# One more feature group by seven products, its first differences on VectorE, and two moved steps, in a fused attention and GLU kernel

## The chip, the cores and the metric

The kernel runs on one core of a Trainium2 chip. The metric is the device time of one execution in microseconds, lower is better. The engines are called by the profile's names: PE (TensorE matmuls), DVE (VectorE), ACT (ScalarE), POOL (GpSimd) and SP, whose queue issues most of the transfers.

## The reference

```python
# x 2048 x 640; wqkv 640 x 1920; wo 640 x 640; w_gate, w_up 640 x 1536; w_down 1536 x 640
xn = layernorm(x)
q, k, v = heads(xn @ wqkv)                  # 32 heads of 20
idx = pos[:, None] - 2 * arange(8)          # 8 taps, two positions apart
a = softmax(where(idx >= 0, q . k[idx] / sqrt(20), -1e9))
s = (sum over taps of a * v[idx]) @ wo
g = silu(((xn @ w_gate) * (xn @ w_up)) @ w_down)
out = x + s * g
```

All of it is fp32.

## The kernel before

**Products.** An fp32 product is three fp32r matmuls: both operands are split into a high part (ACT copies it to fp32r) and a low part (POOL or DVE subtracts it: `split`, L114 and L115), and high x high, high x low and low x high are added. The normalized x lies transposed in `xT[chunk]`, four chunks of 512 positions, five blocks of 128 rows. Weights of gate and up come in 12 feature groups of 128.

**Plain and by seven products.** A plain gate and up for one feature group and one chunk (`gate_up`, L124) is 30 matmuls of 128x128 by 512. `group(f, c0, second)` (L1292) takes gate and up for the pair of chunks c0 and c0 + 1 together by a 2x2 scheme with seven products instead of eight, on four of the five blocks of x, with the fifth added: 54 matmuls, in the order j = 0, 5, 2, 1, 4, 3, 6 with 6, 9, 6, 9, 6, 9, 9 of them. It needs sums and differences on both sides. On x's side these are T1 to T4 for chunks 2 and 3 (`differences(0)` and `differences(1)`, lines L1162 to L1167, on POOL, and `last_difference`, L1188); those of chunks 0 and 1 were made earlier and stored (t_scr and e_scr, loaded again at L1148 and L1152). On the weights' side they are S1 to S4 and d5: `w_add` (L1238, POOL) and `w_split` for the blocks G, S, R, U (640, 768, 384 and 384 columns, ACT and POOL), each in one buffer that the group before must have left. The weights themselves come by `load_wf` (L180, SP).

After a product, ACT's `hold` (L1261) copies its bank where the next product adds to it; DVE adds the other banks to what was held: gate_a (L1274), gate_b (L1264), up_a (L1277); up_b (L1267) and h_b (L1270) are between two held tiles, on DVE for chunks 2 and 3 of feature groups from `VEC` = 2 on, otherwise on POOL. The result h goes to memory (L1250).

**Order.** Every engine runs its instructions in the order in which the code is written. First come layernorm, the transposes, the q, k, v products of the first head group and some gate and up; then the products of the other head groups (L434); then the groups for f = 2 to 10, each for chunks 2 and 3 and then for 0 and 1; f = 11 goes by a group for chunks 0 and 1 and plain for 2 and 3 (f = 0 and 1 are plain on all chunks, two of these products between the first and the second head group). Then `pair_product` (L996) makes s from the attention output and wo, and `product` (L866) the down projection. `places` and `beside` are tables that hang steps behind the n-th product of a group.

**Attention** on 32 heads in 12 units of head group and half runs beside the products: DVE multiplies q by the keys of a tap (L542), reduces (L549), does the softmax with ACT's exponential (L571), multiplies by the values (L508), and POOL or DVE adds (L514). It is a generator which `advance` draws on: each stretch of products grants a credit, each step of attention costs some, and what is granted sets where in the written order its instructions stand. The credit is not a time. Whatever is left at the place `beside[(10, 0, 5)]`, behind the sixth product of the group for f = 10 on chunks 2 and 3, is written out there at once by `advance(1e9)`. Behind it the output goes to memory (`store_o`, L590), the output weights are loaded (`load_wo`, L703), summed by DVE (`sums_wo`, L906 to L909) and split by ACT and POOL (`split_wo`).

**The last stage.** `product(m)` needs sums of h (`sum_h`, L813 to L821), their high and low parts (`hi_h`, `lo_h`, L829), made by DVE and ACT a few products ahead, and DVE gathers what a product gives (`gather`, L882, L886, L889).

Of the kernel before, what the change touches and what calls it, by code (L numbers as in the profile page):

```python
# [29 lines left out]
TPC = CH // P  # L30
# [26 lines left out]
def kernel(  # L57
# [1059 lines left out]
    early_high(1)  # L1117
# [7 lines left out]
    split_wq(1, nc.gpsimd)  # L1125
    gate_up(1, 2)
    gate_up(0, 3)
    gate_up(1, 3)

    f0, f1 = KF - 2, KF - 1  # L1130
    F_TWO = 2
# [24 lines left out]
    def differences(k):  # L1156

        def x(ch, a, m):
            return xT[ch][a][:, 2 * m + k, :].bitcast(F32)

        def sums(out, u, v, eng=nc.gpsimd.tensor_sub):
            eng(out, u, v)  # L1162
            yield

        def parts(j, y):
            nc.scalar.activation(t_unit(j, 0, k), y, AF.Copy)
            nc.gpsimd.tensor_sub(t_unit(j, 1, k), y, t_unit(j, 0, k).bitcast(F32))  # L1167
            yield
# [4 lines left out]
        yield from sums(a, a, x(2, 1, 0))  # L1173
        yield from parts("T1", a)
        r1 = st([P, CH], "gh", 5)
        yield from sums(r1, x(3, 0, 1), x(3, 1, 1), nc.gpsimd.tensor_add)
        yield from sums(r0, r1, r0)
        yield from parts("T3", r0)
        yield from sums(r1, r1, a)
        yield from parts("T2", r1)  # L1180
        z = t4[k] = st([P, CH], "gh", 5)
        yield from sums(z, x(2, 0, 1), r1)
        yield from sums(z, z, x(2, 1, 1), nc.gpsimd.tensor_add)
# [69 lines left out]
    def group(f, c0=0, second=0):  # L1253
# [31 lines left out]
        for n, j in enumerate((0, 5, 2, 1, 4, 3, 6)):  # L1285
# [11 lines left out]
            if (second, n) == (1, 6) and (second, n) in places:  # L1297
                places.pop((second, n))(f)
# [45 lines left out]
    def first_parts():  # L1344
        for name in ("S1", "S2", "S3", "d5", "S4"):
            w_add(2, name)
            yield
        w_split(2, "S")
        yield
# [6 lines left out]
    for m, t in ((m, t) for m in range(1, len(MADE)) for t in range(DIL)):  # L1356
# [3 lines left out]
        for i in range(NE):  # L1360
            n = t * NE + i
            if m < last and n == 0:
                load_wq(m + 1, ((0, 2), (2, 4)) if broad else ((0, 3), (3, 5)))
            elif m < last and n in BLOCK:
                split_wq(m + 1, nc.gpsimd, (BLOCK.index(n), BLOCK.index(n) + 1))
            elif broad and n == BLOCK[1] + 1:
                load_wq(m + 1, ((4, 5),))
            if (m, r, i) == (last - 1, 1, 6):
                load_wf(2)
            if (m, n) in W_SUMS:  # L1370
                wd_sum(W_SUMS.index((m, n)))
            qkv(m, r, i)
            if m == last and n == NT - 7:
                staged[:] = [y for y in staged if y is not stage_pk[-1]]
            elif m == last and n == NT - 5:
                load_t(0)
            elif m == last and n == NT - 3:
                w_split(2, "G")
# [13 lines left out]
    w_split(2, "R")  # L1392
    w_sum.pop(2)
    load_wf(3)
# [160 lines left out]
    for m in range(n_prod):  # L1555
# [5 lines left out]
        if m == 1:  # L1561
            hi_h(AHEAD)
            lo_h(AHEAD)
        elif m == 2:
# [5 lines left out]
        after()  # L1570
        if m + AHEAD + 1 < n_prod:
# [55 lines left out]
```

## Time and profile before

| | |
|---|---|
| median of 3 runs | 738.52 us (736.95 to 738.75) |
| the profiled execution | 737.74 us, of which its span is 735.7 |
| clock granted to PE | 0.999 of full speed |
| PE busy | 729.2 us, 99% of the span |
| DVE, POOL, ACT busy | 629.1, 449.4, 301.0 us |
| q, k, v of the second head group begin on PE | 105.0 us |
| the first seven-product group begins | 272.2 us |
| the last one ends | 505.6 us |

A row of a timeline gives the start, the busy time and the engine, then line, operation and tiles; where the engine was idle before it, the idle time and what ended it stand in brackets at the end. "x6" is six instructions that follow each other. Rows of groups of instructions give their count, then busy us and the mean ns of one, then idle time before them.

### The profile page before, as it was taken

To read this page: it belongs to the slowest core of one execution; us is meant where nothing else is said; L and a number is where in the kernel's file an instruction comes from. 1 tells how busy PE (TensorE), PEld (TensorE's weight loads), DVE (VectorE), ACT (ScalarE), POOL (GpSimd) and SP (SyncE) were. 2 spreads that over 40 slices of the span, in tenths; PEclk is the share of its full clock that TensorE was granted. 3 is DMA by queue.
4 is the path that set the end of the run, shared out by engine and by line. 5 is a ranking of instruction groups with operands and counts; after the bars stand their busy time and mean duration, and the time that the engine had idled before them with its cause. 6 is when DMAs were issued, how large, how long until landed. Compare 5 with 4: busy or idle time off the path is not lost.

```text
span 735.7 us, 11056 instructions
## 1 busy us (share of the span) xinstructions
PE 729.2 (99%) x4030; PEld 666.0 (91%) x4030; DVE 629.1 (86%) x729; ACT 301.0 (41%) x561; POOL 449.4 (61%) x383
## 2 busy tenths in 40 slices
PE   9999999999999999999999999999999999999997
PEld 7989989988999998888888887888999999999997
DVE  7676998799796989899989999978899897777775
ACT  5668312323232333233323332334556664444442
POOL 6159919997778889797889969667644630000000
PEclk9999999999999999999999999999999999999999
DMA  8464589889766659461733542277768955555534
GB/s 325 169 204 164 214 291 302 245 257 257 183 192 174 217 194 349 123 198 58 220 92 96 180 143 73 64 229 192 215 201 244 313 221 193 193 193 194 194 108 143
DMA packets 106436, 143.78 MB, mean 195 GB/s; under 512 B 23080, under 2 KB 75556, under 8 KB 106382
## 3 DMA queue, kind: packets, MB, share of 16 engines
q1 hardware_dynamic: 88654, 121.13, 51.8%
q10 hardware_dynamic: 16000, 12.78, 5.4%
q0 software_dynamic: 1728, 9.18, 5.2%
q8 instruction: 31, 0.51, 0.3%
q14 instruction: 23, 0.19, 0.1%
HBM read 94.40 MB, written 55.67 MB: 204 GB/s over the span
## 4 chain that ended last, share of the span: by engine, by line
PE 94%; DVE 3%; issue 1%; POOL 1%; DMA 1%; SPq 0%; ACT 0%; POOLq 0%; DVEq 0%
PE g L1292 15%; PE q L434 11%; PE u L1292 10%; PE u L434 8%; PE g L434 8%; PE q L866 8%; PE u L866 5%; PE q L1292 5%; PE g L124 5%; PE u L124 5%; PE q L996 3%; PE e L866 3%; PE g L866 3%; PE u L996 2%; PE e L996 2%; PE e L434 1%
## 5 line engine op out<-in xcount | busy, mean ns | idle before, releaser
L514 POOL TENSOR_TENSOR o<-o,t 128x960 f32<-128x960 f32 (+1 forms) x66 | 132.8, 2012 | 9.4 <-DVE t L508 8.5
L508 DVE TENSOR_TENSOR t<-e,kv 128x960 f32<-128x960 f32 (+1 forms) x96 | 99.6, 1038 | 16.2 <-POOL o L514 16.2
L542 DVE TENSOR_TENSOR t<-q,kv 128x1920 f32<-128x1920 f32 (+1 forms) x48 | 92.5, 1927 | 3.2 <-DMA kv<-qkv_scr 3.1
L549 DVE TENSOR_REDUCE lg<-t 128x96 f32<-128x1920 f32 (+1 forms) x48 | 92.3, 1924 | 0.2
L434 PE MATMUL q<-s,xc 128*128 128x360 f32 (+1 forms) x450 | 82.9, 334 | 0.1
L1261 ACT ACTIVATE gh<-g 128x512 f32<-128x512 f32 x57 | 34.1, 598 | 112.8 <-PE g L1292 108.0
L115 POOL TENSOR_TENSOR s<-wraw,s 128x384 fp32r<-128x384 f32 (+6 forms) x57 | 68.4, 1214 | 17.9 <-ACT s L114 17.8
L434 PEld LDWEIGHTS q<-s,xc 128*128 128x128 f32 x450 | 74.9, 188 | 4.2 <-ACT xc L314 0.3
L434 PE MATMUL u<-s,xc 128*128 128x360 f32 (+1 forms) x360 | 65.8, 334 | 0.0
L434 PEld LDWEIGHTS u<-s,xc 128*128 128x128 f32 x360 | 60.3, 188 | 2.2
L434 PE MATMUL g<-s,xc 128*128 128x360 f32 (+1 forms) x330 | 61.5, 338 | 0.0
L434 PEld LDWEIGHTS g<-s,xc 128*128 128x128 f32 x330 | 55.7, 188 | 2.6
L1292 PE MATMUL g<-s,s 128*128 128x512 f32 x228 | 58.0, 390 | 0.0
L1292 PE MATMUL u<-xc,s 128*128 128x512 f32 x228 | 57.9, 389 | 0.0
L866 PE MATMUL q<-xc,s 128*128 128x320 f32 x342 | 55.6, 310 | 0.6 <-DVE s L886 0.6
L866 PEld LDWEIGHTS q<-xc,s 128*128 128x128 f32 x342 | 51.5, 188 | 0.8 <-ACT s L847 0.8
L1292 PEld LDWEIGHTS g<-s,s 128*128 128x128 f32 x228 | 42.7, 188 | 9.2 <-ACT gh L1261 0.4
L1292 PEld LDWEIGHTS u<-xc,s 128*128 128x128 f32 x228 | 42.8, 188 | 8.9
L114 ACT ACTIVATE s<-wraw 128x384 fp32r<-128x384 f32 (+6 forms) x58 | 32.6, 581 | 30.3 <-PE g L1292 10.2
L1292 PE MATMUL g<-xc,s 128*128 128x512 f32 x171 | 42.0, 390 | 0.3 <-ACT gh L1261 0.3
L1292 PE MATMUL q<-xc,pk 128*128 128x512 f32 x171 | 41.9, 389 | 0.0
L514 POOL TENSOR_TENSOR o<-t 128x960 f32<-128x960 f32 (+1 forms) x11 | 22.2, 2014 | 28.3 <-DVE t L508 24.9
(332 smaller groups left out, 1561.3 us busy)
## 6 DMA issues: line engine op xcount, KB each, us to landing
h_scr<-gh SPq DMA_DIRECT2D x48, 256.0 KB, 2.6
wraw<-in_wgu SPq DMA_DIRECT2D x11, 640.0 KB, 4.5
kv<-qkv_scr SPq DMA_DIRECT2D x14, 480.0 KB, 5.9
t<-h_scr SPq DMA_DIRECT2D x8, 768.0 KB, 6.2
qkv_scr<-s ACTq DMA_DIRECT2D x17, 360.0 KB, 3.9
kv<-qkv_scr SPq DMA_DIRECT2D x14, 367.5 KB, 6.8
s_scr<-gh SPq DMA_DIRECT2D x16, 320.0 KB, 3.8
gh<-s_scr SPq DMA_DIRECT2D x16, 320.0 KB, 3.9
```

Of the source, the lines that this page charges most:

```text
L114: nc.scalar.activation(hi, raw, AF.Copy)
L115: eng.tensor_sub(lo, raw, hi.bitcast(F32))
L124: nc.tensor.matmul(acc, a, b, start=first and n == 0, stop=last and n == len(runs) - 1)
L434: nc.tensor.matmul(p, xT[(r * NE + i) // TPC][a][:, k, t0:t0 + P], wq[m][b][k], start=n == 0, stop=n == len(runs) - 1, skip_group_check=ac ...
L508: nc.vector.tensor_mul(t.rearrange("p (n d) -> p n d", d=DH), e[:, :, w].unsqueeze(2).to_broadcast([P, NE * nh, DH]), v)
L514: return NE * c * cost, lambda: eng.tensor_add(y, z, t)
L542: nc.vector.tensor_mul(t, q, k)
L549: nc.vector.tensor_reduce(out=lg[:, :, j:j + 2].rearrange("p n a -> p a n"), in_=t.rearrange("p a (n d) -> p a n d", d=DH), op=ALU.add, ax ...
L866: nc.tensor.matmul(p, y[:, i, k], wd_part(name, k, l), start=new and r == 0, stop=r == len(runs) - 1, skip_group_check=True)
L996: nc.tensor.matmul(b, y, w, start=new and r == 0, stop=r == len(runs) - 1, skip_group_check=True)
L1261: nc.scalar.activation(kept[j], b["ACACABA"[j]], AF.Copy)
L1292: nc.tensor.matmul(y, w, x, start=j in (0, 1, 5) and r == 0, stop=r == len(runs) - 1, skip_group_check=True)
```

## The change

Feature group 1 leaves the plain products on chunks 2 and 3 and is done there by `group(1, 2)`, ahead of all other groups; on chunks 0 and 1 it stays plain. So `F_TWO` is 1, and the sums, splits and loads that went with f = 2 go with f = 1. This first group has no second one on chunks 0 and 1 beside it, so what prepares f = 2 hangs behind the seven products of this one alone (`one_places`). The eleven operations of `differences(0)` go from POOL to DVE, and each takes 0.25 of attention's credit; `differences(1)` stays on POOL. The splits of the second q, k, v weights, the load of the third and the casts of `early_high(1)` stand within the first head group's second half, at its sixth product. In the last stage, `sum_h(8)` and `lo_h(7)` go from behind product 3 to behind product 4's own steps, so that the gathering of product 4 stands ahead of them on DVE.

```diff
-    early_high(1)
...
     for i in range(TPC, NE):
         qkv(0, 1, i)
         advance(PACE * 1.9)
-    split_wq(1, nc.gpsimd)
-    gate_up(1, 2)
+        if i == TPC + 1:
+            split_wq(1, nc.gpsimd)
+            load_wq(2, ((0, 2), (2, 4)))
+            early_high(1)
     gate_up(0, 3)
-    gate_up(1, 3)
+    wf_raw.clear()
...
-    F_TWO = 2
+    F_TWO = 1
...
+        eng = nc.gpsimd if k else nc.vector
+        def high(j, y):
+            nc.scalar.activation(t_unit(j, 0, k), y, AF.Copy)
+        def low(j, y):
+            eng.tensor_sub(t_unit(j, 1, k), y, t_unit(j, 0, k).bitcast(F32))
+        def done(n=1):
+            if not k:
+                credit[0] -= 0.25 * n
         r0, a = st([P, CH], "gh", 5), st([P, CH], "gh", 5)
-        yield from sums(r0, x(3, 0, 0), x(3, 1, 0), nc.gpsimd.tensor_add)
-        yield from sums(a, r0, x(2, 0, 0))
+        eng.tensor_add(r0, x(3, 0, 0), x(3, 1, 0))
+        yield done()
+        eng.tensor_sub(a, r0, x(2, 0, 0))
+        yield done()
...
-            if (second, n) == (1, 6) and (second, n) in places:
+            if n == 6 and (second, n) in places and (second or f == F_TWO):
...
-            if m < last and n == 0:
-                load_wq(m + 1, ((0, 2), (2, 4)) if broad else ((0, 3), (3, 5)))
-            elif m < last and n in BLOCK:
+            if 1 < m < last and n == 0:
+                load_wq(m + 1, ((0, 3), (3, 5)))
+            if m < last and n in BLOCK:
...
+    one_places = {(0, 1): sums("S1", "S2"), (0, 2): sums("S3", "d5", "S4"), (0, 3): splits("G"), (0, 4): splits("S"),
+                  (0, 5): splits("R"), (0, 6): splits("U")}
-    for f in range(2, f1):
+    for f in range(F_TWO, f1):
         places.clear()
-        places.update(two_places)
+        places.update(two_places if f > F_TWO else one_places)
         if f == F_TWO:
-            for n in range(3):
-                places[0, n] = lambda f, n=n: load_late(n)
+            places[0, 0] = lambda f: load_late(0)
+            places[0, 2] = lambda f: (load_late(1), w_add(f + 1, "S3", "d5", "S4"))
+        elif f == F_TWO + 1:
+            places[0, 0] = lambda f: load_late(2)
         group(f, 2)
-        group(f, 0, 1)
+        if f > F_TWO:
+            group(f, 0, 1)
...
+        elif m == 4:
+            sum_h(m + AHEAD)
+            lo_h(m + AHEAD - 1)
...
         after()
+        if m == 3:
+            continue
         if m + AHEAD + 1 < n_prod:
             sum_h(m + AHEAD + 1)
```

By instructions: PE has 60 plain matmuls of 512 columns less and 54 of a group more; POOL has 68 - 59 = 9 operations of 128x512 less, and five sums and four splits more for the one feature group more; DVE has 97 - 85 = 12 operations of 128x512 more and a copy less. (In the changed file the group's lines are higher by 18: L1292 is L1310, L1274 L1292, L1264 L1282, L1277 L1295, L1267 L1285, L1270 L1288, L1261 L1279, L1238 L1256, L1250 L1268; lines up to L1113 are the same.)

**POOL around the first groups.** In the kernel before, the next feature group's weights (the raw ones are wraw_2648, the sums wraw_2728) are summed and split behind the gatherings, with this list between the splits of the first group's last blocks (s_2645) and the next group's block G (pk_2595):

```order
L115 TENSOR_TENSOR s_2645<-wraw_2235,s_2645 128x384
L1148 DMA s_2662<-t_scr 128x1536
L1148 DMA s_2664<-t_scr 128x1536
L1148 DMA s_2677<-t_scr 128x1536
L1152 DMA xc_453<-e_scr_112 128x1024
L1152 DMA xc_453<-e_scr_113 128x1024
L514 TENSOR_TENSOR o_2682<-t_942 128x640
L1238 TENSOR_TENSOR wraw_2728<-wraw_2648 128x256
L1238 TENSOR_TENSOR wraw_2728<-wraw_2728,wraw_2648 128x256
L514 TENSOR_TENSOR o_2682<-o_2682,t_942 128x640
```

In the changed kernel the same stretch, from the last split of the first group's blocks (s_2538) to the block G of the next feature group (pk_2491; raw weights wraw_2541, sums wraw_2574), reads:

```order
L115 TENSOR_TENSOR s_2538<-wraw_2129,s_2538 128x384
L1149 DMA s_2555<-t_scr 128x1536
L1149 DMA s_2557<-t_scr 128x1536
L514 TENSOR_TENSOR o_2499<-t_926 128x640
L1256 TENSOR_TENSOR wraw_2574<-wraw_2541 128x256
L1256 TENSOR_TENSOR wraw_2574<-wraw_2574,wraw_2541 128x256
L514 TENSOR_TENSOR o_2499<-o_2499,t_926 128x640
L1149 DMA s_2588<-t_scr 128x1536
L1256 TENSOR_TENSOR wraw_2574<-wraw_2541 128x256
L1256 TENSOR_TENSOR wraw_2574<-wraw_2541 128x128
L1256 TENSOR_TENSOR wraw_2574<-wraw_2541,wraw_2574 128x256
L115 TENSOR_TENSOR pk_2491<-wraw_2541,pk_2491 128x640
```

The list is nearly the same, but in the kernel before two groups of 54 matmuls ran beside it, and here one; two additions of attention (L514) stand among the sums, one more ahead of the split of block S that comes next, and one ahead of the last split.

**DVE at the end of attention.** Before, from the gate addition of the group for f = 10 on chunks 2 and 3 (gh_4156, L1274) to the next one of its gate additions (L1264), attention's products and additions are:

```order
L1274 TENSOR_TENSOR gh_4156<-gh_4156,q_1_68 128x512
L508 TENSOR_TENSOR t_942<-e_70,kv_1033 128x960
L514 TENSOR_TENSOR o_4056<-o_4056,t_942 128x960
L508 TENSOR_TENSOR t_942<-e_70,kv_1033 128x960
L514 TENSOR_TENSOR o_4056<-o_4056,t_942 128x960
L1264 TENSOR_TENSOR gh_4181<-gh_4181,u_4149 128x512
```

In the changed kernel, at the same place (gh_4163, now L1292 and L1282):

```order
L1292 TENSOR_TENSOR gh_4163<-gh_4163,q_1_68 128x512
L508 TENSOR_TENSOR t_926<-e_70,kv_1037 128x960
L514 TENSOR_TENSOR o_4117<-o_4117,t_926 128x960
L508 TENSOR_TENSOR t_926<-e_70,kv_1037 128x960
L514 TENSOR_TENSOR o_4117<-o_4117,t_926 128x960
L508 TENSOR_TENSOR t_926<-e_70,kv_1037 128x960
L514 TENSOR_TENSOR o_4117<-o_4117,t_926 128x960
L508 TENSOR_TENSOR t_926<-e_70,kv_1037 128x960
L514 TENSOR_TENSOR o_4117<-o_4117,t_926 128x960
L508 TENSOR_TENSOR t_926<-e_70,kv_1037 128x960
L514 TENSOR_TENSOR o_4117<-o_4117,t_926 128x960
L1282 TENSOR_TENSOR gh_4188<-gh_4188,u_4156 128x512
```

Two pairs have become five: the last unit of attention is written later against the products by three of its eight taps.

More of the change, by code (lines that the diff above doesn't have):

```diff
@@ L1345, in first_parts @@
         for name in ("S1", "S2", "S3", "d5", "S4"):
-            w_add(2, name)
+            w_add(F_TWO, name)
             yield
-        w_split(2, "S")
+        w_split(F_TWO, "S")
         yield
@@ L1368 @@
             if (m, r, i) == (last - 1, 1, 6):
[L1369 removed]
+                load_wf(F_TWO)
             if (m, n) in W_SUMS:
@@ L1377 @@
             elif m == last and n == NT - 3:
-                w_split(2, "G")
+                w_split(F_TWO, "G")
             if i == 1:
@@ L1391 @@
     step(100)
-    w_split(2, "R")
-    w_sum.pop(2)
-    load_wf(3)
+    w_split(F_TWO, "R")
+    w_sum.pop(F_TWO)
+    load_wf(F_TWO + 1)
     beside.update({(f0, 0, 5): lambda: advance(1e9), (f0, 1, 0): lambda: begin_last(), (f0, 1, 1): lambda: load_pair(0),
```

36 lines of the change are left out of this document (21 added, 15 removed).

## The prediction

> **What bounds the kernel now.** I read the page's busy times and its chain first, then what TensorE (PE) waits for.
>
> ```profile
> PE 729.2 (99%) x4030; PEld 666.0 (91%) x4030; DVE 629.1 (86%) x729; ACT 301.0 (41%) x561; POOL 449.4 (61%) x383
> PE 94%; DVE 3%; issue 1%; POOL 1%; DMA 1%; SPq 0%; ACT 0%; POOLq 0%; DVEq 0%
> PE q L866 <- DVE s L886: 0.6, 1, 0.6
> PE g L1292 <- ACT gh L1261: 0.3, 1, 0.3
> ```
>
> PE is busy for 729.2 of 735.7 us and carries 94% of the chain that ended last, so two things alone move the end: fewer matmuls, and waits that appear or vanish on PE. Once the kernel is under way it waits twice for another engine, 0.6 and 0.3 us. The other engines count only where they make PE wait, so the work is to find, for each part of the change, the instruction of PE that needs it and by how much it is early.
>
> Next I read PE's timeline in the seven-product groups, which gives the price of a matmul and of a group.
>
> ```profile
> 284.44 1.52 PE L1292 MATMUL g<-xc,pk 128*128 128x512 f32 x6
> 285.80 2.20 PE L1292 MATMUL q<-xc,pk 128*128 128x512 f32 x9
> 296.68 1.52 PE L1292 MATMUL g<-xc,pk 128*128 128x512 f32 x6
> ```
>
> Six matmuls take 1.36 us from start to start, 0.227 each, and a group of 54 takes 12.24. Called G below: the start of the first group, 272.20 in the profile.
>
> **Matmuls: -1.36 us.** Sixty matmuls of 512 columns go (two plain chunks of 30) and 54 come: six times 0.227, all on PE and so on the path. PE reaches the second q, k, v stage 60 x 0.227 = 13.6 us sooner, and the first group begins at about 272.2 - 13.6 = 258.6.
>
> **The first differences on DVE: 0.** Eleven operations of 128x512 come to DVE, between attention.
>
> ```profile
> L1267 DVE TENSOR_TENSOR gh<-gh,gh 128x512 f32<-128x512 f32 x9 | 14.1, 1570 | 0.0
> L508 DVE TENSOR_TENSOR t<-e,kv 128x640 f32<-128x640 f32 x32 | 26.1, 816 | 6.0 <-POOL o L514 6.0
> 140.00:272.00 132.00, 132.00 (x742) 125.02 (x741) 114.65 (x103) 37.89 (x74) 108.32 (x77) 1.00 0.77 218
> ```
>
> The nearest row of that shape with both operands in SBUF is L1267 at 1570 ns; the attention product L508, a quarter larger and also with both operands there, takes 816 ns. Eleven operations are therefore between about 11 x 0.65 = 7.2 (816 scaled by 512/640) and 17.3 us. The last row is the table by stage, its columns after the length being PE, weight loads, DVE, ACT and POOL: from 140 to 272 DVE has 132 - 114.65 = 17.4 us of idle time, and it covers either end. I take the lower, since L508 stands between additions of POOL as these will, and nothing on the path. If the cover is gone, the differences push attention back, to the flush spoken of below.
>
> [...]
>
> **Third q, k, v weights sooner: 0.** The splits of the second weights now stand on POOL ahead of its casts.
>
> ```profile
> 81.42 0.62 POOL L616 CAST kv<-kv 128x512 fp32r<-128x512 f32 x1
> 89.17 4.39 POOL L115 TENSOR_TENSOR s<-wraw,s 128x1080 fp32r<-128x1080 f32 x3
> ```
>
> Before, they end at 93.56, too late for a stage that now begins at 105.0 - 13.6 = 91.4; the casts ahead of them take 89.17 - 81.42 = 7.75 us, so without these they end near 85.8. On SP's queue the stores of the casts now stand behind the weights' load, and the casts end 4.4 us later; a second unit of attention may start so much later, which the DVE idle time above covers. A loss would be the 2.2 us by which the splits missed 91.4, a gain is excluded, since PE waits there for nothing now.
>
> **The weights of feature group 2: +2.2 us.** Formerly a feature group had two seven-product groups, 24.48 us, in which POOL prepared the next one's weights. The new first group has one, 12.24 us, and in it POOL has the same five sums, four splits and the seventh's additions, with attention between them, as the order given with the change shows.
>
> ```profile
> 273.46 0.94 ACT L114 ACTIVATE s<-wraw 128x384 fp32r<-128x384 f32 x2 [0.60 <-ACT s L448]
> 276.89 0.35 SPq L180 DMA_DIRECT2D wraw<-in_wgu  x1
> wraw<-in_wgu SPq DMA_DIRECT2D x11, 640.0 KB, 4.5
> 277.76 1.64 POOL L1148 DMA_DIRECT2D s<-t_scr  x3
> 281.40 1.57 POOL L514 TENSOR_TENSOR o<-t 128x640 f32<-128x640 f32 x1 [0.94 <-DVE t L508]
> 282.94 0.73 POOL L1238 TENSOR_TENSOR wraw<-wraw 128x256 f32<-128x256 f32 x1
> 291.12 1.56 POOL L115 TENSOR_TENSOR pk<-wraw,pk 128x640 fp32r<-128x640 f32 x1
> 294.20 1.85 POOL L115 TENSOR_TENSOR s<-wraw,s 128x768 fp32r<-128x768 f32 x1
> 297.55 1.98 POOL L115 TENSOR_TENSOR s<-wraw,s 128x384 fp32r<-128x384 f32 x2
> ```
>
> I count from G with the pitch of each row. ACT's copy for the last split is done at G + 1.7 (273.46 + 0.47 for one of two), the two splits of 384 last to G + 3.7, and the load of the next weights, which waits for the first of them, is issued at G + 2.8 and lands 4.5 later, at G + 7.3. POOL meanwhile issues two gatherings and adds once for attention, to G + 6.3, and waits for the load. Two sums (0.7 each) to 8.7, one addition (1.53) to 10.2, one gathering (0.55), three sums (two of 0.7, the middle one half as wide) to 12.6, the split of 640 to 14.2. PE's second group wants that low part four matmuls in, at 12.24 + 0.91 = 13.15: 1.0 late. The split of 768 comes after one more addition, at 17.5, wanted at 16.55; the second of 384, after another, at 21.0, wanted 29 matmuls in, at 12.24 + 6.57 = 18.8: 2.2 late. These are one queue, so the delay is the largest, 2.2. Bounds: 0, if the load lands early or additions come out of the way; 4.5, if each of the three additions also waits for DVE as the row at 281.40 does (0.94). I take the count. What is late next is the pair of gatherings of x behind it (issued near G + 26.5 and wanted near G + 37), which fits.
>
> **The last chunk of attention: +3.4 us.** The order moves attention later: after the third-last gate addition DVE has five pairs of product and addition (L508, L514) to flush, formerly two.
>
> ```profile
> 472.30 1.52 PE L1292 MATMUL g<-s,s 128*128 128x512 f32 x6
> 478.47 0.68 DVE L1274 TENSOR_TENSOR gh<-gh,q 128x512 f32<-128x512 f32 x1
> 479.07 1.15 DVE L508 TENSOR_TENSOR t<-e,kv 128x960 f32<-128x960 f32 x1
> 481.33 1.15 DVE L508 TENSOR_TENSOR t<-e,kv 128x960 f32<-128x960 f32 x1
> 483.81 0.68 DVE L1264 TENSOR_TENSOR gh<-gh,u 128x512 f32<-128x512 f32 x1
> 483.91 0.36 SPq L590 DMA_DIRECT2D o_scr<-o  x1
> 486.71 2.24 SPq L703 DMA_DIRECT2D t<-in_wo  x4
> 492.06 1.39 DVE L906 TENSOR_TENSOR kv<-t 128x640 f32<-128x640 f32 x1 [5.17 <-DMA t<-in_wo]
> 506.96 0.68 DVE L1264 TENSOR_TENSOR gh<-gh,u 128x512 f32<-128x512 f32 x1
> 507.79 1.75 POOL L1270 TENSOR_TENSOR gh<-gh,gh 128x512 f32<-128x512 f32 x1 [3.49 <-issue]
> 519.75 1.76 POOL L115 TENSOR_TENSOR s<-t,s 128x640 fp32r<-128x640 f32 x1
> 522.00 1.04 PE L996 MATMUL u<-s,xc 128*128 128x320 f32 x6
> ```
>
> A pair is (483.81 - 479.07)/2 = 2.37 us; three more are 7.1. DVE came to this place 478.47 - 472.30 = 6.2 us behind PE. DVE's instructions between two gate additions, each by the mean of its row in the trace, come to 199 us over the 17 groups of the new order ahead of this place (208 us of PE), formerly to 191 over 16 (196); so it has some 4 us more play, of which waits for ACT and POOL take a part, and I estimate 4.5 behind (between 3 and 6.2); PE's own wait of 2.2 above gives DVE perhaps half of it. The flush then ends 7.1 - 1.7 - 1.1 = 4.3 us later against PE. Behind it hangs a chain with little play: SP's store of the attention output waits for the flush, the load of the output weights stands behind it in the same queue, and DVE already sits idle for 5.17 us until that lands. From there its list runs on without a gap to 506.96, POOL waits 3.49 for this, and then splits one block after another until 519.75 + 1.76 = 521.51; PE uses the last in the third matmul after 522.00, near 522.4. The play is 0.9, so PE waits 4.3 - 0.9 = 3.4. Bounds: 0 if DVE has caught up at the flush, 7.1 - 0.9 = 6.2 if its lag stays 6.2 and PE's wait gives it nothing back. I take the value between, as an estimate.
>
> **A gathering sooner: -0.6 us.** Before the wait at L886, DVE did this:
>
> ```profile
> 596.26 0.48 DVE L882 TENSOR_TENSOR s<-u,gh 128x320 f32<-128x320 f32 x1
> 596.66 1.23 DVE L813 TENSOR_TENSOR s<-s,wraw 128x768 f32<-128x768 f32 x1
> 597.81 0.94 DVE L829 TENSOR_TENSOR s<-wraw,s 128x768 fp32r<-128x768 f32 x1
> 598.68 0.47 DVE L886 TENSOR_TENSOR s<-lg,q 128x320 f32<-128x320 f32 x1
> ```
>
> L886 moves ahead of L813 and L829, 2.0 us, more than the 0.6 that PE waited. L829 is then 0.4 later (one L886) and may be wanted itself: 0 is the other end. The wait of 0.3 behind an exponential in ACT's queue may go, or another hold may meet one; 0, from -0.3 to +0.8 (0.3 of the row, and one more of the longest kind, near 0.5).
>
> **The sum.** -1.36 + 2.2 + 3.4 - 0.6 = +3.6 us. The profiled execution took 737.74 us for its span of 735.7; it lies 0.8 under the median of the three runs, 738.52, inside their spread. 737.74 + 3.6 = 741.3. A time between 736.3 and 740.7 (0.3%, 2.2 us about the median) couldn't be told from no change.
>
> **Rivals.** *POOL, freed, covers both waits.* The eleven differences leave POOL, where the nearest row of that shape, L1270's, took 1.75, so up to 19 us, and L508 alone waited 6.0 us for POOL's additions in the narrow units; with POOL ahead, attention and the sums are done in time, and only -1.36 - 0.6 is left: 735.8, faster. For it speaks that idle time, and DVE's 17.4 us; against it that POOL's list in the first group can't begin before PE has left the buffers, at G + 1.7, and that the five pairs stand behind the gate addition however early DVE is. It decides where the flush ends under 0.9 us later against PE, and the last split at or before G + 18.8. *Only the weights are late*: -1.96 + 2.2 = +0.2, 738.0, the same; it is the case if DVE's lag at the flush is under 1 us; the trace shows it at 6.2 there. *Only attention is late*, with nothing given back by the first wait: -1.96 + 4.5 = +2.5, 740.3, the same; the load of the weights would have to land 2 us sooner than its median. *The differences cost their upper price*: DVE, its 17.4 us used up, brings all its lag to the flush, 6.2 in place of 3.4, 744.1. [...]
>
> **How the numbers follow.** Both waits 0.45 (739.6 to 743.4), only the weights 0.17, only attention 0.13, POOL covers both 0.15, the upper price 0.10. The likeliest gives 741.3; the range reaches from the case without waits, 735.6, to the upper price, 744.6. Faster holds the first rival, 0.15; the same both single waits and the lower edge of the first case (0.08), 0.38; slower the rest, 0.47.
>
> **What would show it.** Right: in the changed kernel PE waits for POOL's split of the weights in the second group, near 271 to 278; the flush of five pairs lies on DVE, the load of the output weights follows it by some 3 us, and PE waits for the last of POOL's splits near 523; no wait stands at the gathering of product 4. Wrong: PE goes through both places without a gap, or DVE comes to the flush less than 2 us behind PE. A wait of PE between 91 and 258, for q, k, v weights, a unit of attention or a bank that ACT hadn't emptied, is in none of the terms.

## The result, and the profile after

The changed kernel takes 743.58 us (median of five, 742.54 to 746.25), the kernel before in the same series 737.57 (736.95 to 738.75): a ratio of 1.0084, 95% interval 1.0060 to 1.0107. It is slower, by 6 us. The profiled execution took 743.58 us for a span of 741.8, against 735.7 before.

The page's busy times after:

```profile
PE 729.6 (98%) x4024; PEld 664.4 (90%) x4024; DVE 627.2 (85%) x740; ACT 305.9 (41%) x568; POOL 444.4 (60%) x383
```

Six matmuls fewer, and yet PE sits idle for 12 us where it was 6.5. What PE waits for, after (us in total, times, longest; L1310 are the seven-product groups, L434 the q, k, v products, L124 a plain product; the wait at the start, which before has too, is left out):

```profile
PE g L1310 <- POOL pk L115: 1.5, 1, 1.5
PE g L124 <- DVE gh L1295: 1.2, 1, 1.2
PE q L434 <- ACT s L448: 1.1, 1, 1.1
PE g L1310 <- ACT gh L1279: 0.8, 2, 0.4
PE u L1310 <- POOL s L115: 0.8, 1, 0.8
```

I laid the two traces side by side from start to start of PE's matmuls; a pause between two starts is a little longer than the idle time printed (1.40 against 1.13 at 243.56). How much later the changed kernel is, in us, place by place: start-up 0.47 (both kernels are the same there); a wait in the last q, k, v stage 1.40; the matmuls -1.36; the second seven-product group (feature group 2 on chunks 2 and 3), 16.13 long instead of 12.24, +3.89; the fourth (feature group 3 on the same chunks), 13.61 long, +1.37; waits for holds that before had and after hasn't, -0.82; the wait at 515 +1.45; the gathering in the last stage -0.81. That is 5.59, and 0.4 at the tail make the 6.0 between the spans (6.1 as they are rounded above).

**The second group.** After, the timeline of POOL (L1256 the sums of weights, L115 the splits, L514 attention's additions), of PE, and of the hold that stood last:

```profile
268.20 0.74 POOL L1256 TENSOR_TENSOR wraw<-wraw 128x256 f32<-128x256 f32 x1 [1.20 <-DMA wraw<-in_wgu]
273.66 1.53 POOL L115 TENSOR_TENSOR pk<-wraw,pk 128x640 fp32r<-128x640 f32 x1
275.15 1.55 POOL L514 TENSOR_TENSOR o<-o,t 128x640 f32<-128x640 f32 x1
275.24 0.73 PE L1310 MATMUL g<-xc,pk 128*128 128x512 f32 x2 [1.46 <-POOL pk L115]
280.98 0.99 POOL L115 TENSOR_TENSOR s<-wraw,s 128x384 fp32r<-128x384 f32 x1
282.02 0.50 PE L1310 MATMUL u<-xc,s 128*128 128x512 f32 x1 [0.80 <-POOL s L115]
283.25 0.60 ACT L1279 ACTIVATE gh<-u 128x512 f32<-128x512 f32 x1 [3.20 <-POOL gh L1285]
293.85 0.74 POOL L1256 TENSOR_TENSOR wraw<-wraw 128x256 f32<-128x256 f32 x1 [3.55 <-DMA wraw<-in_wgu]
```

POOL works from 268.20 on without a pause. Its split of the next block G ends at 275.2, four matmuls into PE's second group, and PE goes on at once; its last split ends at 281.97, and so does PE's second wait. Both splits are behind additions of attention. A hold of ACT then waits for POOL's up_b of the first group (L1285), which stands behind the same splits. So does the load of the raw weights for feature group 3, since it is queued on SP behind the store of h that waits for POOL: POOL is idle for 3.55 until that load lands, and the fourth group is late too.

**The wait at 243.6** has no counterpart before. Rows of the changed kernel, from the place where its cause stands; L768 is a 960 KB transfer inside memory issued by POOL, L590 the store of attention's output, L452 a store of q, k, v issued by ACT, L448 ACT's copy that frees a bank of PE:

```profile
202.42 0.56 POOL L768 DMA_DIRECT2D w_scr<-w_scr  x1
205.30 1.20 SPq L590 DMA_DIRECT2D o_scr<-o  x2
216.24 2.25 POOL L514 TENSOR_TENSOR o<-t 128x960 f32<-128x960 f32 x1 [6.65 <-DMA o_scr<-o]
238.32 1.01 SPq L590 DMA_DIRECT2D o_scr<-o  x2
242.42 0.52 ACTq L452 DMA_DIRECT2D qkv_scr<-s  x1
243.56 2.67 PE L434 MATMUL q<-s,xc 128*128 128x360 f32 x15 [1.13 <-ACT s L448]
```

and of the kernel before, with the size and landing time of its store from the table of transfers, and then that of the changed kernel:

```profile
200.93 1.00 SPq L590 DMA_DIRECT2D o_scr<-o  x2
208.64 2.25 POOL L514 TENSOR_TENSOR o<-t 128x960 f32<-128x960 f32 x1 [0.30 <-DVE t L508]
219.23 0.56 POOL L768 DMA_DIRECT2D w_scr<-w_scr  x1
238.72 0.47 ACT L448 ACTIVATE s<-q 128x360 f32<-128x360 f32 x1 [4.25 <-DMA o_scr<-o]
o_scr<-o SPq DMA_DIRECT2D x1, 320.0 KB, 4.8
```

```profile
o_scr<-o SPq DMA_DIRECT2D x1, 320.0 KB, 10.1
```

Before, the transfer goes 18 us behind the store; after, 3 us ahead of it, since the transfer went out 16.8 us sooner with its q, k, v stage and the store 4.4 us later. The store then takes 10.1 us instead of 4.8. The output tile `o` has one buffer, so POOL's first addition of the next unit waits 6.65 us for the store, DVE's products wait for POOL (5.61 at 218.52), and this unit's own store goes out only at 238.32. Its second part is issued at 238.75 and lands 3.6 us later, at 242.34. In the trace ACT's issue at 242.42 waits for the semaphore on which that landing is counted, and the copy that frees PE's bank stands behind this issue in ACT's queue: it ends at 243.51, and PE goes on at 243.56. Before, the copy in the same place waits for such a store too, at 238.72, but PE wants the bank only at 241.00.

**The end of attention**, after: the flush of five pairs on DVE, what SP loads behind it, and PE's wait.

```profile
478.73 0.68 DVE L1292 TENSOR_TENSOR gh<-gh,q 128x512 f32<-128x512 f32 x1
490.97 0.68 DVE L1282 TENSOR_TENSOR gh<-gh,u 128x512 f32<-128x512 f32 x1
494.87 2.20 SPq L703 DMA_DIRECT2D t<-in_wo  x4
499.59 1.37 DVE L906 TENSOR_TENSOR kv<-t 128x640 f32<-128x640 f32 x1 [4.56 <-DMA t<-in_wo]
514.66 0.68 DVE L1295 TENSOR_TENSOR gh<-gh,g 128x512 f32<-128x512 f32 x1
515.39 3.74 PE L124 MATMUL g<-xc,s 128*128 128x512 f32 x15 [1.18 <-DVE gh L1295]
```

PE's group starts at 473.82, before at 468.89. DVE comes to gate_a 4.91 behind that start (before 478.47 - 468.89 = 9.58), and the flush ends 17.15 behind it (before 483.81 - 468.89 = 14.92). So it is 2.2 later against PE, although it is three pairs, 7.1, longer. What PE waits for is DVE's up_a at 514.66, which frees a bank. Before, up_a ended at 508.98 and PE started there at 509.04, so it had no play; POOL's last split ends at 527.85, about a microsecond before PE uses it.

### The profile page after: what moved, and what is told of

Its sections match the earlier page's. It is cut to its first block, busy times and chain, and to the rows that moved or that the text cites. A ratio compares the mean times of both kernels' runs of the same rounds, so it can differ in the third digit from the quotient of the medians.

```text
span 741.8 us, 11069 instructions
## 1 busy us (share of the span) xinstructions
PE 729.6 (98%) x4024; PEld 664.4 (90%) x4024; DVE 627.2 (85%) x740; ACT 305.9 (41%) x568; POOL 444.4 (60%) x383
## 5 line engine op out<-in xcount | busy, mean ns | idle before, releaser
L514 POOL TENSOR_TENSOR o<-o,t 128x960 f32<-128x960 f32 (+1 forms) x66 | 133.5, 2023 | 10.8 <-DVE t L508 9.9
L508 DVE TENSOR_TENSOR t<-e,kv 128x960 f32<-128x960 f32 (+1 forms) x96 | 99.8, 1039 | 23.5 <-POOL o L514 23.4
L434 PE MATMUL q<-s,xc 128*128 128x360 f32 (+1 forms) x450 | 83.0, 334 | 1.9 <-ACT s L448 1.1
L115 POOL TENSOR_TENSOR s<-wraw,s 128x384 fp32r<-128x384 f32 (+6 forms) x60 | 71.3, 1202 | 22.4 <-ACT s L114 22.4
L1279 ACT ACTIVATE gh<-g 128x512 f32<-128x512 f32 x60 | 35.9, 599 | 115.6 <-PE g L1310 107.0
L434 PEld LDWEIGHTS q<-s,xc 128*128 128x128 f32 x450 | 74.9, 188 | 6.1 <-ACT s L448 1.4
L434 PE MATMUL u<-s,xc 128*128 128x360 f32 (+1 forms) x360 | 65.8, 334 | 0.0
L1310 PE MATMUL u<-xc,s 128*128 128x512 f32 x240 | 61.8, 391 | 0.9 <-POOL s L115 0.8
L434 PEld LDWEIGHTS u<-s,xc 128*128 128x128 f32 x360 | 60.3, 188 | 2.3
L434 PE MATMUL g<-s,xc 128*128 128x360 f32 (+1 forms) x330 | 61.5, 337 | 0.0
L1310 PE MATMUL g<-s,s 128*128 128x512 f32 x240 | 61.0, 389 | 0.0
L434 PEld LDWEIGHTS g<-s,xc 128*128 128x128 f32 x330 | 55.7, 188 | 2.6
L1310 PEld LDWEIGHTS u<-xc,s 128*128 128x128 f32 x240 | 44.9, 188 | 11.7 <-POOL s L115 1.7
L1310 PEld LDWEIGHTS g<-s,s 128*128 128x128 f32 x240 | 45.0, 188 | 9.3
L114 ACT ACTIVATE s<-wraw 128x384 fp32r<-128x384 f32 (+6 forms) x61 | 34.7, 584 | 33.9 <-PE g L1310 10.4
L1310 PE MATMUL g<-xc,s 128*128 128x512 f32 x180 | 44.4, 391 | 0.8 <-ACT gh L1279 0.8
L1310 PE MATMUL q<-xc,pk 128*128 128x512 f32 x180 | 44.1, 389 | 0.0
L1310 PEld LDWEIGHTS g<-xc,s 128*128 128x128 f32 x180 | 33.6, 188 | 8.8 <-ACT gh L1279 1.9
```

Source lines behind the costliest of these rows:

```text
L114: nc.scalar.activation(hi, raw, AF.Copy)
L115: eng.tensor_sub(lo, raw, hi.bitcast(F32))
L434: nc.tensor.matmul(p, xT[(r * NE + i) // TPC][a][:, k, t0:t0 + P], wq[m][b][k], start=n == 0, stop=n == len(runs) - 1, skip_group_check=ac ...
L508: nc.vector.tensor_mul(t.rearrange("p (n d) -> p n d", d=DH), e[:, :, w].unsqueeze(2).to_broadcast([P, NE * nh, DH]), v)
L514: return NE * c * cost, lambda: eng.tensor_add(y, z, t)
L1279: nc.scalar.activation(kept[j], b["ACACABA"[j]], AF.Copy)
```

## The experiments

Theory A, from the traces: the loss is made of (1) POOL's list in the single first group, (2) the output store that meets a bulk transfer, and (3) the longer flush. Rival B: the differences on DVE cost more than their cover; rival C: the change of order in itself, whatever the transfer.

**The gathering alone**, put into the kernel before:

```diff
+        elif m == 4:
+            sum_h(m + AHEAD)
+            lo_h(m + AHEAD - 1)
...
+        if m == 3:
+            continue
```

> The kernel before, with the gathering of product 4 alone moved ahead of sum_h(8) and lo_h(7). Theory A (each wait of PE is its own): PE's wait at L866 for L886 (0.57 us, 0.8 with the slow restart) goes and nothing comes for it: 0.6 to 0.9 us faster, 736.7 to 737.0. Rival: lo_h(7), now 0.4 later, is wanted in its place: no change within 0.3.

737.70 us against 738.14, ratio 0.9994 (0.9985 to 1.0003). The wait at L886 is in no row of what PE waits for. The gain of the row, 0.6, fits, but the interval reaches from -1.1 to +0.2 us; by time it is open.

**The transfer later** (changed kernel):

```diff
-    W_SUMS = ((1, 2), (1, 12), (2, 4), (2, 12), (3, 7))
+    W_SUMS = ((1, 2), (1, 12), (2, 4), (2, 12), (3, 13))
```

> The changed kernel, with the last sum of the down weights in memory (a 960 KB transfer, issued by POOL at 202.4) hung behind the 13th in place of the 7th product of its stage, near 217, so that it no longer runs beside the store of the attention output at 205.3. Theory A: that store lands in 3 to 5 us and not 10.1, POOL's addition behind it waits under 2 us and not 6.65, the exponential at 235.6 comes some 5 us sooner, and PE's wait for ACT L448 at 243.6 (1.4 us) goes: 1.0 to 1.8 us faster than the changed kernel, 741.8 to 742.6; the waits at 275 and 282 stay. Rival B (the differences on DVE alone make attention late): the wait at 243.6 stays, no change.

740.82 us, ratio 1.0031 (1.0020 to 1.0043). Timeline and transfers of this kernel, at the places shown above:

```profile
211.27 2.25 POOL L514 TENSOR_TENSOR o<-t 128x960 f32<-128x960 f32 x1 [2.51 <-DVE t L508]
233.88 1.01 SPq L590 DMA_DIRECT2D o_scr<-o  x2
o_scr<-o SPq DMA_DIRECT2D x1, 320.0 KB, 3.8
```

The store lands in 3.8 us, the addition no longer waits for it, the exponential that the expectation names comes 4.4 sooner, the next store too (233.88 instead of 238.32), and the wait at 243.6 is gone. The waits in the second group (1.10 and 1.06) and at the flush (1.45) stay. Between the two spans part (2) is worth 2.6 us: its own wait of 1.4, and 1.2 by which the second and the fourth group are less late (15.49 and 13.09 long).

**The differences back on POOL** (changed kernel; attention gets the credit back):

```diff
-        eng = nc.gpsimd if k else nc.vector
+        eng = nc.gpsimd
...
-            if not k:
-                credit[0] -= 0.25 * n
```

> The changed kernel, with the first differences back on POOL and no credit taken for them. Theory A: the waits of PE in the second group (275 and 282) depend on POOL's list of the first group and stay, 2.5 to 3.9 us; only the wait at 243.6 and some of the tail move: 741 to 744. Rival B (the differences on DVE make attention late and so all the waits): the waits at 243.6, 275 to 287, 308 to 313 and 515 go, 736 to 738.

750.93 us, ratio 1.0176 (1.0155 to 1.0197). What PE waits for most:

```profile
PE u L1309 <- POOL s L115: 3.8, 3, 2.1
PE g L1309 <- POOL pk L115: 3.4, 2, 2.5
```

Rival B is refuted: the differences on DVE, taken together with their credit, save some 7 us here, and what grows without them is POOL's list, part (1). The output store meets the transfer here too (transfer at 203.46, store at 203.55, its 320 KB land in 12.8 us), so the meeting doesn't come from the differences on DVE.

**One unit's additions on DVE** (the unit that runs in the first groups):

```diff
+            if u == ORDER[5]:
+                eng = nc.vector
```

> The changed kernel, with the additions of the one unit of attention that runs beside the first groups (7 of 128x640) on DVE in place of POOL, in the same order. Theory A: POOL's list of the first group is 3 additions (4.6 us) shorter, so the splits of feature group 2 end near 272 (block G), 274 (S) and 276 (U) against 275.2, 278.5 and 282.0, and PE's waits of 1.7 and 1.1 us there, and the holds behind POOL's up_b and h_b (1.0 and 1.4 us), go: 3 to 5 us faster than the changed kernel, 738.5 to 740.5; some comes back if the tail, which these waits had relieved, is late by more than 1.45 us. Rival (the load of the weights, landing at 268.2, sets the splits, not the additions): the wait at 275 stays at over 1 us, and under 1.5 us are won.

750.63 us, ratio 1.0165 (1.0152 to 1.0179). PE's waits for POOL's splits shrink to 0.3 in all, as A says; but the price on DVE was far above what I expected. Timeline:

```profile
270.73 8.33 DVE L516 TENSOR_TENSOR o<-o,t 128x640 f32<-128x640 f32 x1
286.14 3.49 PE L1312 MATMUL g<-xc,s 128*128 128x512 f32 x9 [3.07 <-ACT gh L1281]
```

One addition, mostly 0.83 us elsewhere in the same unit, took 8.33 while POOL ran eight instructions back to back from 270.0 to 278.4. DVE's gate additions came late, POOL waited for them, the holds for POOL, and PE for the holds (6.4 us in four waits); over the 4 us behind the two long ones PE's granted clock was 0.61 and 0.64.

**Without the feature group** (changed kernel, feature group 1 plain on all chunks as before; the other three parts stay):

```diff
-    F_TWO = 1
+    F_TWO = 2
```

> The changed kernel without its feature group: F_TWO = 2 again, feature group 1 plain on chunks 2 and 3; the differences on DVE, the weights sooner and the gathering stay. Theory A: 6 matmuls come back (+1.36), and with the first group's full 24.5 us for the next weights the waits of PE at 275 to 287 and 308 to 313 (3.9 and 1.4 us) go, as does the meeting of transfer and store at 205 (1.4), since the later stages begin 12 us later again: 736.5 to 739. Rival (the rest of the change, the differences on DVE or the moved weights, carries the loss): 741 or more.

741.20 us, ratio 1.0042 (1.0029 to 1.0054): a miss, since it lies in the range of the rival. The waits at 243 and at the flush are gone, but a new one stands at 299.8. Timeline, and a table by stretch (the granted clock is the third number from the end):

```profile
281.17 1.10 POOL L1154 DMA_DIRECT2D xc<-e_scr  x2
281.26 0.38 SPq L590 DMA_DIRECT2D o_scr<-o  x1
293.35 1.56 POOL L514 TENSOR_TENSOR o<-t 128x640 f32<-128x640 f32 x1 [9.49 <-DMA o_scr<-o]
299.80 0.73 PE L1311 MATMUL g<-xc,pk 128*128 128x512 f32 x2 [1.84 <-POOL pk L115]
299.80:304.80 5.00, 5.00 (x15) 3.96 (x16) 5.00 (x7) 0.60 (x1) 5.00 (x4) 0.66 0.02 5
```

It is part (2) at another place. In the kernel before this store went out at 275.91, ahead of POOL's loads at 277.76, and landed in 3.4 us; here it goes out behind them and lands in 12.0. POOL stands for 9.49 us, its split is late, PE waits 2.1 by starts, and the clock of 0.66 behind it costs another 1.6.

**No attention in the first group** (with the later transfer), then with a higher rate in the later groups:

```diff
-            advance(PACE * len(runs) * (GROUP_RATE if two(f) else 0.184))
+            advance(PACE * len(runs) * (0.0 if f == F_TWO else GROUP_RATE if two(f) else 0.184))
```

> The changed kernel with the late transfer, and no credit for attention in the first group, so that none of its additions stands on POOL between the weights' sums and splits there (and none on DVE either). Theory A: POOL ends the split of block U near 274 (279.6 with the additions), and PE's waits for it (1.1 and 1.1 us) and behind its up_b and h_b (0.7 and 0.8) go, 3.5 us; but attention is written about two products later, with 7 pairs in the flush, so the wait at 513 grows from 1.4 by up to 4.7 us: 738 to 743 against 740.8. Rival (the landing of the weights at 266 alone decides): the waits at 273 and 280 stay above 0.7 us each.

> The same as e6, with the credit of the other groups at 0.2 in place of 0.184, so that only three pairs are left for the flush. Theory A: the waits at 273 to 285 go as in e6 and the tail's wait at 513 goes or stays under 1.4, unless DVE can't do what is written into the groups and its gate additions come over 8 us behind PE: 736.5 to 739.5, 1 to 4 us faster than e6. Rival (how far DVE has come, not what is written where, sets the flush's end): the wait at 513 is as in e6, within 1 us.

756.50 us (ratio 1.0250, 1.0236 to 1.0264), and with `GROUP_RATE = 0.2` 751.51 (1.0192, 1.0170 to 1.0215). In both, the second group runs in 12.24 us without a wait: with no additions of attention in it, POOL's list fits, which is part (1). The additions have to go somewhere, though. Both times are far above what I expected. In the first of the two the additions make the flush longer, and in the second DVE lags in several groups, so that exponentials come late and holds stand behind them in ACT's queue (what PE waits for, the first row of the one and of the other):

```profile
PE u L1310 <- ACT gh L1279: 12.1, 1, 12.1
```

```profile
PE g L1310 <- ACT gh L1279: 11.9, 5, 5.3
```

**up_b and h_b of feature group 1 on DVE** (`VEC = 1`, with the later transfer):

> The changed kernel with the late transfer and up_b and h_b of the first group on DVE in place of POOL. Theory A: the waits for the splits at 273 and 280 (1.1 and 1.1) stay, since those two stand behind the splits; the holds that waited for POOL's up_b and h_b (0.7, and 0.8 in the group after the next) go: 0.5 to 1.5 us faster than with the late transfer alone, 739.3 to 740.3. Rival (DVE, which waits for POOL's additions itself, does them no sooner): the holds wait as before, 740.3 to 741.5.

745.19 us, ratio 1.0094 (1.0078 to 1.0109), 4 us above the kernel it was made from: PE's waits for POOL's last splits went from 0.8 to 2.3, those for holds from 1.1 to 2.2. DVE came to up_a 9.8 us behind PE in the first group. The trace shows why:

```profile
273.01 7.29 DVE L1285 TENSOR_TENSOR gh<-gh,gh 128x512 f32<-128x512 f32 x1
```

The moved up_b itself, 0.68 us at its next turn, took 7.29 while POOL ran without a pause from 272.94 to 279.74, like the addition of 8.33 above.

**The pair of x loads behind the store** (the kernel without the feature group; SP issues them two products later):

```diff
-        nc.gpsimd.dma_start(xT[ch][a][:, 0:2, :], e_scr[n])
+        nc.sync.dma_start(xT[ch][a][:, 0:2, :].bitcast(F32), e_scr[n])
...
+            places[0, 4] = lambda f: load_late(2)
```

> Edit: the changed kernel without the added feature group (F_TWO = 2), in which the pair of gatherings of x (e_scr, the third load_late) is issued by SP behind the fifth product instead of by POOL behind the third, so that less bulk data stands in front of attention's output store. Theory A (the loss of that kernel comes from the store meeting POOL's bulk loads, POOL's first addition on the one output tile waiting 9.5 us, and PE's clock dropping behind PE's 2.1 us wait): POOL's wait for the store shrinks below 6 us, PE's wait at 300 goes or falls under 0.8, and the time falls from 741.2 to 737 to 739.5. Rival (the three loads of t_scr are enough to hold the store, or the waits come from attention's order alone): wait and time stay, 740.5 to 742.

739.37 us, ratio 1.0016 (1.0008 to 1.0025): 1.8 less than with these loads ahead of the store. Timeline:

```profile
290.47 1.57 POOL L514 TENSOR_TENSOR o<-t 128x640 f32<-128x640 f32 x1 [7.57 <-DMA o_scr<-o]
```

POOL waits 7.57 instead of 9.49, not under 6 as I expected, and the store still takes 9.2 us; the three t_scr loads ahead of it and the x loads right behind it are what it still meets. PE's wait at 300, and the slow matmuls behind it, are gone (six of them take 1.37 by starts from 300.23, and 1.95 from 303.45 with the loads ahead of the store), and a smaller wait of 1.0 by starts came at 304.5. Of the 3.2 us by which the kernel without the feature group is slower than the kernel before, this gives back 1.8. The other 1.4 aren't taken apart; POOL's long wait for the store is still among them.

**The five gatherings issued by SP** (with the later transfer):

```diff
-        nc.gpsimd.dma_start(tt[0][n], t_scr[:, 3 * n:3 * n + 3])
+        nc.sync.dma_start(tt[0][n].bitcast(F32), t_scr[:, 3 * n:3 * n + 3])
...
-        nc.gpsimd.dma_start(xT[ch][a][:, 0:2, :], e_scr[n])
+        nc.sync.dma_start(xT[ch][a][:, 0:2, :].bitcast(F32), e_scr[n])
```

> Edit: the kernel with the late w_scr transfer, whose five gatherings around the first seven-product groups (t_scr three times, e_scr twice) are issued by SP instead of by POOL. Nothing else moves. Theory A (in the first group POOL's list is too long by about 1.1 us): three issues of 0.55 us leave POOL's list ahead of the splits, PE's waits of 1.10 and 1.06 at 273 and 280 shrink to under 0.4 each and the holds behind them shrink too; 738.3 to 740.2. Rival (the splits are late for the load of the raw weights, or for ACT, not for the length of POOL's list): the waits stay; 740.5 to 741.5. The wait at 513 behind the flush of five pairs stays at about 1.4 in both.

740.33 us, ratio 1.0032 (1.0021 to 1.0044), no different from the kernel it was made from (1.0031), and between the two forecasts. Against the first group's start the splits end 0.8 sooner; the wait at block G, by its one pause, shrank from 1.0 to 0.2, that at the last split stayed at 0.95, since PE, no longer held up at the first, comes to it sooner too. The second group is 0.75 shorter, and the fourth gives this back, 13.87 long instead of 13.09. POOL's timeline:

```profile
266.15 0.74 POOL L1256 TENSOR_TENSOR wraw<-wraw 128x256 f32<-128x256 f32 x1 [1.48 <-DMA wraw<-in_wgu]
278.39 0.99 POOL L115 TENSOR_TENSOR s<-wraw,s 128x384 fp32r<-128x384 f32 x1
291.54 0.74 POOL L1256 TENSOR_TENSOR wraw<-wraw 128x256 f32<-128x256 f32 x1 [4.97 <-DMA wraw<-in_wgu]
```

Of the three issues, 1.65 us, that left the list ahead of the last split, 0.9 went into a longer wait for the raw weights (1.48; 0.57 in the kernel it was made from). From their landing to the end of the last split it is still 13.2 us of work without a pause, three additions of 1.56 among it. And the next raw weights land later, so POOL waits 4.97 for them. So the length of the list is one part of the answer and the landing of the weights another, as the rival said.

**A shorter flush** (the kernel just told, `GROUP_RATE = 0.188`):

> Edit: the run before this one with GROUP_RATE = 0.188 instead of 0.184; in the written order the first groups stay the same, and the flush behind the third-last gate addition has three pairs instead of five. Theory A (PE waits at 513 for the length of the flush): two pairs of 2.37 us less, and the wait of 1.4 at 513 goes, time 1 to 1.8 us under the run before it (736.8 to 739). Rival (DVE, given more attention ahead of the flush, comes to it later by as much, since it has no idle time left): the wait stays and the time is the same or up to 1 us longer.

745.38 us, ratio 1.0098 (1.0084 to 1.0112), 5 us above it. The wait at the flush did go, as A says, and the pairs moved forward cost more than it gave. PE's waits for POOL's last splits and for holds, in the whole kernel, were 1.1 and 0.8 us and are now

```profile
PE u L1310 <- POOL s L115: 2.9, 3, 1.6
PE g L1310 <- ACT gh L1279: 2.1, 3, 1.2
```

Four groups between the first ones and the flush, which run in 12.24 us each in the kernel just told, are longer by 5.3 us together. Neither theory had said that.

**The kernel before, with its transfer early**:

```diff
-    W_SUMS = ((1, 2), (1, 12), (2, 4), (2, 12), (3, 7))
+    W_SUMS = ((1, 2), (1, 12), (2, 4), (2, 12), (3, 0))
```

> Edit: the kernel before, with its fifth w_scr transfer (960 KB, issued by POOL) moved from the product (3, 7) to (3, 0), so that it is issued some 2 us ahead of attention's output store at 201 instead of 18 us behind it. Nothing else moves. Theory A (a store that meets this transfer lands late and the single output tile stops POOL's queue): the store lands in 8 to 11 us instead of 4.8, POOL's first addition of the next unit waits 2 to 4 us for it (before: 0.3, for DVE), attention in that unit is some 3 us late; whether PE waits depends on its play there, so 737.6 to 739.6. Rival (the wait of 6.65 us in the changed kernel came from attention's place in the order, not from the transfer): the store lands in about 5 us, the addition doesn't wait, 737.3 to 738.3.

739.90 us, ratio 1.0025 (1.0016 to 1.0033). Timeline, and the store's landing:

```profile
198.78 0.83 POOL L768 DMA_DIRECT2D w_scr<-w_scr  x1
201.92 1.05 SPq L590 DMA_DIRECT2D o_scr<-o  x2
211.32 2.25 POOL L514 TENSOR_TENSOR o<-t 128x960 f32<-128x960 f32 x1 [3.23 <-DMA o_scr<-o]
o_scr<-o SPq DMA_DIRECT2D x1, 320.0 KB, 8.8
```

Nothing of the change is in this kernel, and the store lands in 8.8 us instead of 4.8 and POOL waits 3.23 us for it. Rival C falls: the meeting alone does it. The profiled execution was the shortest of its eleven, 738.47, and its span is 0.6 us longer than before's, with a wait of PE of 0.5 us for a late load of t_scr in the second group; where the rest of the 1.9 us goes, the trace doesn't show.

No version was clearly faster than the kernel before.

## Why the prediction was right or wrong, by its steps

Direction and range hold, and so do both places: slower, 743.58 inside 735.6 to 744.6, with PE waiting in the second group and behind the flush. The value was 2.3 us low, just above the 743.4 up to which the likeliest case reached, and three steps inside it were off.

- *Matmuls, -1.36*: measured so.
- *First differences, 0*: right, and of rival B's upper price nothing is left. One of the changed kernel's groups of instructions:

```profile
L1168 DVE TENSOR_TENSOR s<-gh,s 128x512 fp32r<-128x512 f32 x3 | 3.6, 1214 | 0.0
```

  The eleven took 10.3 us together, between my bounds of 7.2 and 17.3 (single ones from 0.67 to 1.99), and with them back on POOL the time is 7 us longer. My upper bound rested on one row, L1267's 1570 ns, and the price it stands for didn't come. The addition of 8.33 us and the up_b of 7.29 in later runs went far beyond that row, each as a single instruction.
- *Third q, k, v weights, 0*: right. POOL's splits of the second weights end at 86.4 (predicted 85.8), and PE's stage begins at 91.87 with no wait.
- *Weights of the next feature group, +2.2*: the place, the queue and the reason were right (block G was forecast at G + 14.2 and ended at G + 14.7; the last split at G + 21.0 and ended at G + 21.5), the size was not. Taking the two latenesses as one delay was right: the two waits at the splits, 1.73 and 1.07, make 2.8, about the lateness of the last split (21.5 - 18.8 = 2.7). But I stopped at the last split. The group lost 3.89, since 1.09 more came at the holds that wait for POOL's up_b and h_b behind it. And the fourth group lost 1.37, because the next load of weights was queued on SP behind a store that waited for POOL. The step that failed is "what is late next ... fits": the loads of x did fit, but up_b, h_b and the load behind the store weren't counted.
- *The last chunk of attention, +3.4*: over-sized; it was 1.45. I had DVE 4.5 us behind when it came to the flush, and at least 3; it was 1.5 behind, the end of the product it adds being at 477.2. That is less than the 2 us which the prediction names as a sign that it is wrong, so this step failed. I gave part of PE's waits to DVE for catching up, but the lag doesn't follow them: with the later transfer the first groups lose 4.1 us and DVE is 1.3 behind, with `VEC = 1` they lose 7.9 and it is 1.5 behind. What sets it stays open. The flush came 2.2 later, not 4.3, and of these 2.2 DVE made up 0.8 by up_a, since the sums L908 and L909 took 1.6 us together and before 4.0, although L907 waited 1.7 us longer for its load. And the wait stands at DVE's gate addition up_a at 515, not at POOL's last split, where I had looked for it.
- *Gathering, -0.6*: -0.81 in the pair of traces. *Holds, 0* (-0.3 to +0.8): -0.82, outside. I took the idle time of 0.3 that the view lists; by starts two of before's groups were 0.29 and 0.57 longer than 12.24 for late holds, and both are 12.24 now.
- *In none of the terms*: the wait at 243.6, 1.40. The prediction names that stretch as the place where it would be wrong. I moved a stage by 13.6 us and counted each queue it was moved past, but not that a transfer of this stage would now go out ahead of a store of attention, which isn't in its queue.

The errors were 3.1 us too low on the weights, 1.95 too high on attention, and 1.4 that I hadn't seen: that the sum came near is partly luck, since they offset each other.

## What to carry to other kernels

When a stage is moved against work that runs beside it, list the bulk transfers of both and look which now overlaps a small store or load whose buffer somebody needs back; a single-buffered tile turned 5 us of a slower landing into a wait of 6.65 us in POOL's queue here. When an engine's list is late for one consumer, follow it to the end of its list and to the loads queued behind it, not to the first consumer. And in this kernel, whose DVE is 85% busy, work taken out of one place to shorten it showed up in another: four of the twelve versions removed the wait they aimed at and were slower for others.

## What the runs showed of the hardware that I had not expected

PE's granted clock fell behind some of its waits. Of all of PE's waits over 0.9 us behind the first 15 us of these traces, none up to 1.58 us was followed by a lower clock (1.00 over the next 4 us, 15 waits). Of the nine between 1.84 and 12.1 us seven were, by the mean over the next 4 us: 0.68 behind 1.84 (without the feature group), 0.64 and 0.61 behind 2.67 and 3.07 (one unit's additions on DVE), 0.60 and 0.50 behind 2.29 and 12.1 (no attention in the first group), 0.67 and 0.50 behind 3.21 and 5.29 (the same with the higher rate). The waits of 2.07 and 2.52 in the kernel with the differences on POOL were not: 1.00 behind both. In the row at 299.80 a wait of 1.84 us cost 1.6 more that way. So in these traces a wait of some 2 us cost 1.6 us more or nothing; its length alone doesn't tell which, and what does isn't shown.

The 320 KB stores told of above landed in 3.4 to 4.8 us with no bulk transfer just ahead of them, and took 8.8 to 12.8 when POOL had issued one up to 3.6 us ahead. Not every store issued behind one was slow. In the changed kernel an earlier store of attention goes out at 171.30, just behind another 960 KB transfer, and isn't slowed (the same store took 6.0 us before, with no such transfer ahead of it):

```profile
171.22 0.77 POOL L768 DMA_DIRECT2D w_scr<-w_scr  x1
o_scr<-o SPq DMA_DIRECT2D x1, 480.0 KB, 4.6
```

By the trace's packets the store's queue moved first there, from 172.7, and POOL's packets began at 175.1, 3.9 us behind their issue; at 202.42 they began after 2.1 us, ahead of the store, whose queue then moved nothing until 209.7. These are few cases, and no run here changes this gap alone.

And three DVE instructions took many times their usual length beside a POOL that ran back to back: the addition of 8.33 us (mostly 0.83 in that unit), the up_b of 7.29 (0.68 at its next turn), and an up_b of 5.00 in the kernel with the shorter flush. POOL was busy for all but 0.5 to 0.7 us of each of them. L508, the same operation on DVE, never took over 1.16 us in its 96 turns in the changed kernel; what decides between the two isn't shown.
